# Transposing the result on VectorE, loading the up weights in two pieces, and starting the load buffers on a 4096-byte boundary

## The chip, the cores and the metric

The kernel runs on one core of one Trainium2 chip. The metric is the device time of one execution in microseconds (us). Each run also runs the kernel before on the same chip, in the same rounds. Ratios in this document are the mean time of one kernel's fast runs over the mean of the other's fast runs of the same rounds, so a ratio is not quite the ratio of the medians that are quoted. Intervals are 95%. The fast executions of one kernel scatter in two groups: in the rounds of the first four experiments the kernel before took 412.2 to 412.4 us seven times and 413.0 to 413.2 us four times. How many of each group a mean holds can move it by some tenths of a us.

Names in the profiles: PE is TensorE, the matrix engine, PEld its weight loads, DVE is VectorE, ACT ScalarE, POOL GpSimd, SP SyncE (here it issues the loads); a q after a name (SPq) is the queue of that engine. SBUF is the on-chip memory of 128 partitions into which the loads go, PSUM the memory into which PE writes. The granted clock is the share of TensorE's full clock that the throttle allowed.

## The reference

One decoding step of a transformer block for one token: attention over a long K/V cache, then a gated feed-forward layer. Everything is bf16 in memory.

```
x: (1, 1, 1024)   k_cache, v_cache: (1, 4, 65536, 128)   32 query heads, 4 K/V heads
wq: (1024, 4096)  wo: (4096, 1024)  w_gate, w_up: (1024, 3584)  w_down: (3584, 1024)

h  = x + attention(layernorm(x), k_cache, v_cache, wq, wo)
h2 = h + (gelu(layernorm(h) @ w_gate) * (layernorm(h) @ w_up)) @ w_down
```

The two caches are 134 MB of the 173 MB that have to be read, and each byte is used once. So the kernel can be no faster than its loads.

## The kernel before

All large loads go through one helper, into a rotating pool of five buffers of 32 KiB per partition, issued on one queue in the order of their use. A load can be issued when the load five places ahead of it has been used up.

```python
    CW = 16384
    NBUF = 5
    const = ctx.enter_context(tc.tile_pool(name="const", bufs=1))
    small = ctx.enter_context(tc.tile_pool(name="small", bufs=2))
    chpool = ctx.enter_context(tc.tile_pool(name="chpool", bufs=NBUF))
    # ... (cut)
    def load(src, name):
        t = chpool.tile([P, CW], BF16, name=name, tag="ch")
        n, w = src.shape[1], src.shape[2]
        tv = t[:, 0:n * w].rearrange("p (n w) -> p n w", w=w)
        nc.sync.dma_start(out=tv, in_=src)
        return tv
```

Pools lie in SBUF in the order in which they are opened. `const` and `small` come first, so the load buffers begin at byte 23552 of each partition (23 x 1024, or 5.75 x 4096). K is transposed on PE, bf16 pairs at a time as fp32, and multiplied with the queries; V is multiplied with the softmax.

```python
            for b in range(NB2):                                     # K, 4 transposes into one PSUM bank
                m0 = b * 8 + c * 2 + hf
                nc.tensor.transpose(out=kt_ps[:, b, :], in_=k32s[m0 // 16][:, m0 % 16, :], identity=ident_f[:])
            # ... (cut)
            nc.tensor.matmul(acc[32 * c:32 * c + rep * TG, :],       # V, 512 columns at a time
                             lhsT=pTs[a // HG][:, a % HG, :, :].rearrange("p r t -> p (r t)"),
                             rhs=v_sb[:, i * TG:(i + 1) * TG, :].rearrange("p t d -> p (t d)"), # ... (cut)
```

The last stages: the up weights are loaded in pieces of 4, 3 and 1 of the 8 row blocks, the down weights in pieces of 14, 7, 4, 2 and 1 of 28. The result lies as 128 partitions by 8 columns and has to become 8 rows of 128 for the store.

```python
    for j0, nj, src in up_proj(B_w_up, "wu", [GB] * (DC // GB - 1) + [GB - 1, 1]):    # 4, 3, 1
        # ... (cut)
    h2_cp = rows.tile([P, DC], F32, name="h2_cp")
    nc.vector.tensor_tensor(out=h2_cp[:], in0=dl_ps[:], in1=hd_cp[:], op=ALU.add)
    h2T_ps = ps_t.tile([DC, P], F32, name="h2T_ps", tag="T")
    nc.tensor.transpose(out=h2T_ps[:], in_=h2_cp[:], identity=ident_f[:])
    o_row = rows.tile([DC, P], BF16, name="o_row")
    nc.vector.tensor_copy(out=o_row[:], in_=h2T_ps[:])
    nc.sync.dma_start(out=out[0, 0].rearrange("(c p) -> c p", p=P), in_=o_row[:])
```

## Time and profile before

| | before |
|---|---|
| time, median of the first 3 runs | 412.27 us |
| span of the profiled run | 410.5 us |
| HBM bytes read, mean rate over the span | 173.02 MB, 422 GB/s |
| PE busy | 73% of the span |
| one 4 MiB load, mean from the first K landing to the last V landing | 9.82 us |
| last load landed | 406.9 us |
| last addition to issue of the store | 0.99 us |

These are lines of the page of the kernel before. In the strips each character is one of 40 equal slices; a digit is a busy share in tenths, PEclk the clock granted to TensorE, GB/s what the DMA engines moved.

```profile
span 410.5 us, 6349 instructions
PE 297.7 (73%) x2705; PEld 195.3 (48%) x2705; DVE 167.6 (41%) x292; ACT 168.0 (41%) x281; POOL 5.1 (1%) x16
...
DMA  8999999999999999999999999999999999999994
...
q8 instruction: 21, 0.34, 0.3%
...
HBM read 173.02 MB, written 0.00 MB: 422 GB/s over the span
```

DMA is at 9 in every slice but the first and the last, PE is not.

The next view is the chain of waits of the kernel before, from 300 us on: start, duration, and what the chain passed through.

```profile
311.41 25.09 DMA v_sb<-in_A_v_cache_dram
...
372.76 25.63 DMA wd_sb<-in_B_w_down_dram
398.39 0.04 issue
398.43 3.20 PE d_ps L358 x28
401.63 0.02 issue
401.66 0.70 DVE d_r L465
402.36 0.04 issue
402.40 1.86 PE hd_cp_ps L387 x8
404.27 3.06 PE dl_ps L460 x112
```

The last V load lands at 311.41 + 25.09 = 336.50 us and the first down-weight load at 398.39. From there PE is nearly always at work, and it finishes the narrow `dl_ps` matmuls at 407.33, a little after the last bytes land. Then comes the tail, here as the timeline shows it (start, duration, engine, line, operation):

```profile
407.35 0.17 DVE L468 TENSOR_TENSOR h_cp<-dl_ps,hd_cp 128x8 f32<-128x8 f32 x1 [2.87 <-PE dl_ps L460]
...
407.57 0.38 PE L470 MATMUL h2T_ps<-ident_f,h_cp 128*8 128x128 f32 x1 [0.26 <-DVE h_cp L468]
407.99 0.28 DVE L472 CAST o_row<-h2T_ps 8x128 bf16<-8x128 f32 x1 [0.47 <-PE h2T_ps L470]
408.34 0.35 SPq L473 DMA_DIRECT2D out_dram<-o_row  x1
```

### The profile page before, as it was taken

What the parts mean: (1) busy time and instruction counts of PE and PEld (TensorE: products, weight loads), DVE (VectorE), ACT (ScalarE), POOL (GpSimd) and SP (SyncE); (2) the same over time, 40 slices, a digit from 0 to 9 for tenths busy, and PEclk for the clock granted to TensorE, in tenths of its full rate; (3) what the DMA queues carried; (4) which work ended last, traced back from release to release, by engine and by line L of the source; (5) the groups of instructions that cost most, each with busy time, mean ns of one, the idle gap of its engine ahead of it and who ended that gap; (6) DMA issues with size and microseconds to landing.
All of it is one profiled execution on the core that took longest, in us unless ns stands there. A gap on an engine that the chain in (4) does not pass through costs nothing.

```text
span 410.5 us, 6349 instructions
## 1 busy us (share of the span) xinstructions
PE 297.7 (73%) x2705; PEld 195.3 (48%) x2705; DVE 167.6 (41%) x292; ACT 168.0 (41%) x281; POOL 5.1 (1%) x16
## 2 busy tenths in 40 slices
PE   0438989889688987496988929888987466466546
PEld 0216656655365654464565617465654223163225
DVE  0213565557256545265556535456545101021011
ACT  0013766653855654733655634455754700000000
POOL 1100000000000000000000000000000001000000
PEclk9986999999999999599999966999999585568565
DMA  8999999999999999999999999999999999999994
GB/s 358 409 460 407 460 408 457 407 454 414 439 428 429 434 417 449 416 449 410 449 420 441 423 441 426 431 433 426 437 426 437 422 445 422 434 430 433 429 418 174
DMA packets 6828, 173.43 MB, mean 422 GB/s; under 512 B 912, under 2 KB 912, under 8 KB 1296
## 3 DMA queue, kind: packets, MB, share of 16 engines
q1 hardware_dynamic: 6640, 173.02, 98.1%
q8 instruction: 21, 0.34, 0.3%
q14 instruction: 7, 0.06, 0.0%
q10 hardware_dynamic: 160, 0.00, 0.0%
HBM read 173.02 MB, written 0.00 MB: 422 GB/s over the span
## 4 chain that ended last, share of the span: by engine, by line
PE 51%; DMA 20%; DVE 14%; issue 8%; ACT 6%; POOL 0%; SPq 0%; POOLq 0%; ACTq 0%; DVEq 0%
PE kt_ps L220 26%; PE qk_ps L245 11%; DMA k_sb<-in_A_k_cache_dram 7%; DMA wd_sb<-in_B_w_down_dram 6%; DMA v_sb<-in_A_v_cache_dram 6%; DVE sc_sb L256 5%; PE acc_ps L300 5%; ACT pT L283 4%; PE sct_ps L253 4%; DVE mx L257 4%; DVE kt_sb L227 3%; ACT qk_sb L250 2%; PE o_ps L316 1%; PE wg_ps L160 1%; PE d_ps L358 1%
## 5 line engine op out<-in xcount | busy, mean ns | idle before, releaser
L220 PE MATMUL kt_ps<-ident_f,k_sb 128*128 128x128 f32 x1024 | 148.1, 288 | 17.4 <-DVE kt_sb L227 13.0
L225 ACT COPY kt_sb<-kt_ps 128x1024 bf16<-128x1024 bf16 x116 | 116.4, 1013 | 91.7 <-PE kt_ps L220 63.0
L220 PEld LDWEIGHTS kt_ps<-ident_f,k_sb 128*128 128x128 f32 x1024 | 117.5, 147 | 55.5 <-issue 21.3
L227 DVE COPY kt_sb<-kt_ps 128x1024 bf16<-128x1024 bf16 x140 | 94.6, 687 | 76.1 <-PE qk_ps L245 42.6
L245 PE MATMUL qk_ps<-kt_sb,qsel 128*32 128x512 bf16 x512 | 65.1, 395 | 7.7 <-DVE kt_sb L227 7.7
L256 DVE COPY sc_sb<-sct_ps 128x512 f32<-128x512 f32 x32 | 34.2, 1068 | 46.1 <-PE sct_ps L253 43.7
L283 ACT ACTIVATE pT<-sc_sb,nbias 128x256 bf16<-128x256 f32 x64 | 31.5, 493 | 20.6 <-DVE nbias L275 20.6
L300 PE MATMUL acc_ps<-v_sb,pT 128*32 128x512 bf16 x512 | 33.7, 407 | 3.7 <-DMA v_sb<-in_A_v_cache_dram 3.7
L250 ACT COPY qk_sb<-qk_ps 128x512 f32<-128x512 f32 x32 | 18.8, 589 | 24.9 <-PE qk_ps L245 16.5
L245 PEld LDWEIGHTS <-qsel 128*32 128x32 bf16 x512 | 15.1, 94 | 26.2 <-issue 23.8
L253 PE MATMUL sct_ps<-ident_f,qk_sb 128*128 128x128 f32 x128 | 19.9, 278 | 8.6 <-ACT qk_sb L250 8.6
L300 PEld LDWEIGHTS <-pT 128*32 128x32 bf16 x512 | 14.7, 102 | 18.5 <-issue 7.1
L257 DVE TENSOR_REDUCE mx<-sc_sb 128x8 f32<-128x512 f32 x32 | 22.0, 686 | 1.0
L253 PEld LDWEIGHTS sct_ps<-ident_f,qk_sb 128*128 128x128 f32 x128 | 14.3, 140 | 13.6 <-ACT qk_sb L250 13.6
L167 ACT COPY wg_ev<-wg_ps 96x512 f32<-96x512 f32 x1 | 0.6, 581 | 45.9 <-PE wg_ps L160 45.9
L309 PE MATMUL l_ps<-lpart,ones_f 128*128 128x8 f32 x16 | 3.7, 306 | 15.8 <-ACT pT L283 15.8
L358 PE MATMUL at_ps<-wo_sb,o2z 128*32 128x512 bf16 x64 | 7.1, 619 | 8.1 <-DMA wo_sb<-in_A_wo_dram 8.1
L160 PE MATMUL wu_ps<-wu_sb,hnz 128*32 128x512 bf16 x56 | 7.2, 625 | 7.8 <-DMA wu_sb<-in_B_w_up_dram 7.8
L160 PEld LDWEIGHTS <-hnz 128*32 128x32 bf16 x112 | 4.8, 123 | 16.0 <-issue 13.7
L283 ACT ACTIVATION_READ_ACCUMULATOR pT<-sc_sb,nbias 128x1 f32 x64 | 11.9, 187 | 0.0
L167 ACT ACT_TABLE_LOAD x1 | 1.3, 1283 | 25.0 <-DVE q_ev L165 25.0
L309 PEld LDWEIGHTS l_ps<-lpart,ones_f 128*128 128x128 f32 x16 | 3.0, 234 | 17.8 <-ACT pT L283 17.4
(126 smaller groups left out, 98.4 us busy)
## 6 DMA issues: line engine op xcount, KB each, us to landing
k_sb<-in_A_k_cache_dram SPq DMA_DIRECT2D x16, 4096.0 KB, 30.4
v_sb<-in_A_v_cache_dram SPq DMA_DIRECT2D x16, 4096.0 KB, 19.3
wq_sb<-in_A_wq_dram SPq DMA_DIRECT2D x2, 4096.0 KB, 16.7
wo_sb<-in_A_wo_dram SPq DMA_DIRECT2D x2, 4096.0 KB, 29.6
wg_sb<-in_B_w_gate_dram SPq DMA_DIRECT2D x2, 3584.0 KB, 36.4
wu_sb<-in_B_w_up_dram SPq DMA_DIRECT2D x1, 3584.0 KB
wd_sb<-in_B_w_down_dram SPq DMA_DIRECT2D x1, 3584.0 KB, 25.6
wu_sb<-in_B_w_up_dram SPq DMA_DIRECT2D x1, 2688.0 KB, 38.1
```

What stands on the lines that cost most here:

```text
L160: nc.tensor.matmul(banks[s // 4][32 * g:32 * g + 32, :], lhsT=stat, rhs=mov(s), start=first, stop=last, tile_position=(0, 32 * g))
L220: nc.tensor.transpose(out=kt_ps[:, b, :], in_=k32s[m0 // 16][:, m0 % 16, :], identity=ident_f[:])
L225: nc.scalar.copy(out=dst_bf, in_=src_bf)
L227: nc.vector.tensor_copy(out=dst_bf, in_=src_bf)
L245: nc.tensor.matmul(qk_ps[32 * c:32 * c + 32, :], lhsT=qsel[:, g, par, hf, :], rhs=mv[:, :, :, par], start=(hf == 0 and par == 0), stop=(hf ...
L250: nc.scalar.copy(out=qk_sb[:], in_=qk_ps[:])
L253: nc.tensor.transpose(out=sct_ps[:, b, :], in_=qk_sb[:, b * P:(b + 1) * P], identity=ident_f[:])
L256: nc.vector.tensor_copy(out=sl.rearrange("p h (m t) -> p m t h", t=2), in_=src_v)
L257: nc.vector.tensor_reduce(out=st["mx"][:, :, pi], in_=sl, axis=AX.X, op=ALU.max)
L283: nc.scalar.activation(out=pT[:, :, r, :], in_=sc_sb[:, r, hf * HG * TG:(hf + 1) * HG * TG].rearrange("p (a t) -> p a t", t=TG), func=ACT. ...
L300: nc.tensor.matmul(acc[32 * c:32 * c + rep * TG, :], lhsT=pTs[a // HG][:, a % HG, :, :].rearrange("p r t -> p (r t)"), rhs=v_sb[:, i * TG: ...
L358: nc.tensor.matmul(bank[32 * g:32 * g + 32, :], lhsT=stat, rhs=w2[:, s * 512:(s + 1) * 512], start=first, stop=last, tile_position=(0, 32 ...
```

## The change

It has three parts. The result is rounded to bf16 by the last addition, put into a zero-padded 128x32 block, and turned by four 32x32 transposes on VectorE, so that neither PE nor PSUM is needed in the tail. The up weights come in two loads of 4 row blocks. And a new pool `lead`, opened first and filled exactly to byte 20480 (5 x 4096), puts the load buffers, opened second, on a 4096-byte boundary of SBUF.

```diff
+    lead = ctx.enter_context(tc.tile_pool(name="lead", bufs=1))
+    ones_f = lead.tile([P, P], F32, name="ones_f")
     ... (14 more constant tiles move from const to lead)
+    chpool = ctx.enter_context(tc.tile_pool(name="chpool", bufs=NBUF))
     const = ctx.enter_context(tc.tile_pool(name="const", bufs=1))
     small = ctx.enter_context(tc.tile_pool(name="small", bufs=2))
-    chpool = ctx.enter_context(tc.tile_pool(name="chpool", bufs=NBUF))
     ... (cut)
-    for j0, nj, src in up_proj(B_w_up, "wu", [GB] * (DC // GB - 1) + [GB - 1, 1]):
+    for j0, nj, src in up_proj(B_w_up, "wu", [GB] * (DC // GB)):
     ... (cut)
+    o_blk = rows.tile([P, 32], BF16, name="o_blk")
+    nc.vector.memset(o_blk[:], 0.0)
+    o_tr = rows.tile([32, P], BF16, name="o_tr")
     ... (cut)
-    h2_cp = rows.tile([P, DC], F32, name="h2_cp")
-    nc.vector.tensor_tensor(out=h2_cp[:], in0=dl_ps[:], in1=hd_cp[:], op=ALU.add)
-    h2T_ps = ps_t.tile([DC, P], F32, name="h2T_ps", tag="T")
-    nc.tensor.transpose(out=h2T_ps[:], in_=h2_cp[:], identity=ident_f[:])
-    o_row = rows.tile([DC, P], BF16, name="o_row")
-    nc.vector.tensor_copy(out=o_row[:], in_=h2T_ps[:])
-    nc.sync.dma_start(out=out[0, 0].rearrange("(c p) -> c p", p=P), in_=o_row[:])
+    nc.vector.tensor_tensor(out=o_blk[:, 0:DC], in0=dl_ps[:], in1=hd_cp[:], op=ALU.add)
+    for i in range(4):
+        nc.vector.transpose(out=o_tr[:, 32 * i:32 * i + 32], in_=o_blk[32 * i:32 * i + 32, :])
+    nc.sync.dma_start(out=out[0, 0].rearrange("(c p) -> c p", p=P), in_=o_tr[0:DC, :])
```

More of the change, by code (lines that the diff above doesn't have):

```diff
@@ L58 @@
     assert NT % (DCH * CH) == 0 and CH % TG == 0 and CH == 32 and W2 == 16 and DCH % 2 == 0
+    lead = ctx.enter_context(tc.tile_pool(name="lead", bufs=1))
+    ones_f = lead.tile([P, P], F32, name="ones_f")
+    ident_f = lead.tile([P, P], F32, name="ident_f")
+    esel = lead.tile([P, 2, P], BF16, name="esel")
+    qsel = lead.tile([P, Hkv, 2, 2, 32], BF16, name="qsel")
+    hsel = lead.tile([P, 2], F32, name="hsel")
+    sel = lead.tile([P, 32], F32, name="sel")
+    x_pc = lead.tile([P, DC], F32, name="x_pc")
+    x_cp = lead.tile([P, DC], F32, name="x_cp")
+    x_row = lead.tile([DC, P], BF16, name="x_row")
+    ident_bf = lead.tile([P, P], BF16, name="ident_bf")
+    x_pc_bf = lead.tile([P, DC], BF16, name="x_pc_bf")
+    xn_bf = lead.tile([P, DC], BF16, name="xn_bf")
+    neg_half = lead.tile([P, 1], F32, name="neg_half")
+    oT_all = lead.tile([P, Hq], BF16, name="oT_all")
+    xnz = lead.tile([P, DC, 32], BF16, name="xnz")
+    chpool = ctx.enter_context(tc.tile_pool(name="chpool", bufs=NBUF))
     const = ctx.enter_context(tc.tile_pool(name="const", bufs=1))
     small = ctx.enter_context(tc.tile_pool(name="small", bufs=2))
-    chpool = ctx.enter_context(tc.tile_pool(name="chpool", bufs=NBUF))
     ps_m = ctx.enter_context(tc.tile_pool(name="ps_m", bufs=1, space=PSUM))
@@ L83 @@
     assert HD <= CW and DC % WB == 0
-    x_pc_bf = const.tile([P, DC], BF16, name="x_pc_bf")
     nc.scalar.dma_start(out=x_pc_bf[:], in_=A_x[0, 0].rearrange("(p c) -> p c", c=DC))
-    x_row = const.tile([DC, P], BF16, name="x_row")
     nc.scalar.dma_start(out=x_row[:], in_=A_x[0, 0].rearrange("(c p) -> c p", p=P))
@@ L91 @@
         wq_tiles.extend(wv[:, i, :] for i in range(WB))
-    ident_bf = const.tile([P, P], BF16, name="ident_bf")
     make_identity(nc, ident_bf[:])
-    ident_f = const.tile([P, P], F32, name="ident_f")
     make_identity(nc, ident_f[:])
-    ones_f = const.tile([P, P], F32, name="ones_f")
     nc.vector.memset(ones_f[:], 1.0)
-    hsel = const.tile([P, 2], F32, name="hsel")
     nc.vector.memset(hsel[:], 0.0)
@@ L102 @@
         nc.vector.memset(hsel[64 * s:64 * s + 64, s:s + 1], 1.0)
-    neg_half = const.tile([P, 1], F32, name="neg_half")
     nc.vector.memset(neg_half[:], -0.5)
-    sel = const.tile([P, 32], F32, name="sel")
     nc.vector.tensor_tensor(out=sel[:], in0=ident_f[:, 0:32], in1=ident_f[:, 32:64], op=ALU.add)
@@ L108 @@
     nc.vector.tensor_tensor(out=sel[:], in0=sel[:], in1=ident_f[:, 96:128], op=ALU.add)
-    esel = const.tile([P, 2, P], BF16, name="esel")
     for par in range(2):
@@ L140, in layernorm_cols @@
         nc.vector.tensor_scalar(out=dst_bf, in0=xc[:], scalar1=rstd[:, 0:1], scalar2=None, op0=ALU.mult)
-    x_pc = const.tile([P, DC], F32, name="x_pc")
     nc.vector.tensor_copy(out=x_pc[:], in_=x_pc_bf[:])
-    xn_bf = const.tile([P, DC], BF16, name="xn_bf")
     layernorm_cols(x_pc[:], xn_bf[:], "ln1")
@@ L147, with padded @@
     nc.tensor.transpose(out=xT_ps[:], in_=x_row[:], identity=ident_bf[0:DC, 0:DC])
-    x_cp = const.tile([P, DC], F32, name="x_cp")
     nc.vector.tensor_copy(out=x_cp[:], in_=xT_ps[:])
-    def padded(pool, vec, ncols, name):
-        t = pool.tile([P, ncols, 32], BF16, name=name)
+    def padded(pool, vec, ncols, name, t=None):
+        if t is None:
+            t = pool.tile([P, ncols, 32], BF16, name=name)
         nc.gpsimd.memset(t[:], 0.0)
@@ L170 @@
     assert NQ == 8 and D == 1024
-    xnz = padded(const, xn_bf[:], DC, "xnz")
+    padded(None, xn_bf[:], DC, "xnz", xnz)
     q_ps = [ps_qk.tile([P, 512], F32, name="q_ps", tag="qkps") for _ in range(2)]
@@ L185 @@
         nc.tensor.matmul(qsel_ps[:, par, :], lhsT=esel[:, par, :], rhs=qT_bf[:], start=True, stop=True)
-    qsel = const.tile([P, Hkv, 2, 2, 32], BF16, name="qsel")
     nc.vector.memset(qsel[:], 0.0)
@@ L192 @@
                                   in_=qsel_ps[64 * t:64 * t + 64, :, :].rearrange("p a (g h) -> p g a h", h=rep))
-    oT_all = const.tile([P, Hq], BF16, name="oT_all")
     k_v = [A_k_cache[0, g].rearrange("(p n) d -> p n d", p=P) for g in range(Hkv)]
```

## The prediction

> **What bounds the kernel.** The load stream. The page gives the 16 DMA engines 0.9 of every slice but the first and the last, 173.02 MB read at 422 GB/s over a span of 410.5 us. PE, the busiest compute engine, is busy 73%. Landings read from the chain of waits and from the DMA issues: the first K load (third in the queue) lands at 32.21 us, the last V load at 336.50, so 31 loads of 4 MiB took 9.82 us each (427 GB/s). The first down-weight load lands at 398.39: 428 GB/s all the way. The queue does not run dry: no V load took under 14.6 us from issue to landing, over one load's time. The Trainium skill, "DMA: Bandwidth & Descriptors", section "Where 436 GB/s comes from", puts the ceiling of the SBUF ports at 435.2 GB/s; this trace agrees: the wo loads landed 9.66 us apart (434 GB/s).
>
> **The tail.** The last 256 KB land near 406.9 (issue 391.5 plus 15.4). PE runs on to 407.33 (112 narrow matmuls in 3.2 us, clock 0.5). Then by the timeline: add at 407.35, PE transpose of the result 407.57 to 407.95, cast from PSUM 407.99 to 408.27, output DMA issued 408.34, span ends at 410.5.
>
> **What changes.**
> 1. Result transpose. Removed: a PE transpose (0.38 us) and the cast (0.28 us), with hand-overs 0.74 us, all on the critical path. Added: four independent 32x32 transposes on VectorE. Small DVE operations here last 0.16 to 0.18 us, and four independent casts of 64x64 took 0.93 us together, so my estimate is 0.4 to 0.6 us. Gain 0.15 to 0.35 us.
> 2. Up weights in 2 loads instead of 3: the bytes are the same. PE now has 28 matmuls (3.6 us at half clock) after the last up-weight bytes instead of 7, so act_bf comes about 2 us later, near 395.5 instead of 393.6, still ahead of the down weights at 398.4. The first down-weight load is issued near 359 instead of 372.76, but behind the same bytes, so it lands no earlier. Gain 0 to 0.1 us.
> 3. Load buffers begin at byte 20480 (5 x 4096) per partition instead of 23552 (5.75 x 4096). It can only matter through the rate of the DMA writes. The old start is already a multiple of 1024, and wo ran at 434 GB/s into the same unaligned buffers, so a large cost of misalignment is not visible. Upper bound: all K and V loads at 9.66 instead of 9.82 us, 32 x 0.16 = 5 us. Most likely nothing, with a fair chance of 1 to 3 us; 0.7 us on average.
>
> **Predicted time:** 411.0 us, 408.2 to 412.4 eight times in ten. Faster by over 2% (under 404.0) 0.03, within 2% 0.95, slower by over 2% 0.02.
>
> **What would show it.** Step 1: last add to output issue about 0.7 us instead of 1.0. Step 2: wd landings keep their distance to the last V landing; the last wu matmul ends near 393.5. Step 3: the time per 4 MiB load between the first K and the last V landing: 9.82 us if alignment is nothing, 9.70 or less if it counts.
>
> **What would make it wrong.** The DMA write rate depends on the 4096-byte boundary more than wo's rate suggests (gain of 3 to 5 us); a transpose on DVE costs over 0.3 us each in sequence; the later act_bf pushes the last stage past the wd landing.

## The result, and the profile after

The changed kernel took 412.36 us (median of 6 runs, 412.15 to 412.73), the kernel before 412.35 us (median of 6, 412.17 to 413.30). The ratio is 0.9997, interval 0.9984 to 1.001: no difference.

The page after the change, the lines that answer to those of before:

```profile
span 410.4 us, 6350 instructions
PE 296.6 (72%) x2704; PEld 194.9 (47%) x2704; DVE 168.2 (41%) x296; ACT 168.0 (41%) x281; POOL 5.1 (1%) x16
...
DMA  8999999999999999999999999999999999999994
...
q8 instruction: 21, 0.34, 0.3%
```

The load stream is the same. The first K load landed at 32.15 us and the last V load at 336.60, so a 4 MiB load took 304.45 / 31 = 9.82 us on average, to the hundredth what it took before. In both traces 1.213 us is the median time of one 32 KiB DMA packet. Two lines of the chain of waits after the change show the first K load (before: `1.65 30.56`) and the first down-weight load:

```profile
1.64 30.51 DMA k_sb<-in_A_k_cache_dram
...
359.31 38.93 DMA wd_sb<-in_B_w_down_dram
```

The timeline of the last stages after the change:

```profile
389.82 3.51 PE L165 MATMUL wu_ps<-wu_sb,hnz 128*32 128x512 bf16 x28 [5.04 <-DMA wu_sb<-in_B_w_up_dram]
...
395.04 0.20 DVE L444 TENSOR_TENSOR act_bf<-wu_t,gl 128x12 bf16<-128x12 f32 x1
398.29 3.18 PE L361 MATMUL d_ps<-wd_sb,actz 128*32 128x512 bf16 x28 [3.28 <-DMA wd_sb<-in_B_w_down_dram]
...
407.22 0.17 DVE L473 TENSOR_TENSOR o_blk<-dl_ps,hd_cp 128x8 bf16<-128x8 f32 x1 [2.89 <-PE dl_ps L466]
407.42 0.84 DVE L475 STREAM_TRANSPOSE o_tr<-o_blk 32x32 bf16<-32x32 bf16 x4
408.34 0.36 SPq L476 DMA_DIRECT2D out_dram<-o_tr  x1
```

Two things are to be seen. The up matmuls now end at 389.82 + 3.51 = 393.33 and the activation is ready at 395.24, about 1.6 us later than before (393.63), but PE still has to wait for the down weights until 398.29, so this costs nothing. And the four transposes take 0.84 us. The tail from the last addition to the store's issue is 408.34 - 407.22 = 1.12 us, where it was 0.99: it became longer by 0.13 us, and the store goes out at the same 408.34 us because in this run the first down weights were used 0.14 us earlier (398.29 against 398.43).

The chain of waits after the change shows how the four transposes follow one another (in the place of the second one the chain has 0.21 us of VectorE's own queue):

```profile
407.22 0.18 DVE o_blk L473
407.40 0.02 issue
407.42 0.20 DVE o_tr L475
407.62 0.21 DVEq L502
407.83 0.01 issue
407.85 0.20 DVE o_tr L475
408.05 0.01 issue
408.06 0.20 DVE o_tr L475
```

Each lasts 0.20 us and the next starts when the one before is over. They do not overlap, although none depends on another.

### The profile page after: what moved, and what is told of

It is laid out like the page before. It is cut to its first block, busy times and chain, and to the rows that moved or that the text cites. A ratio compares the mean times of both kernels' runs of the same rounds, so it can differ in the third digit from the quotient of the medians.

```text
span 410.4 us, 6350 instructions
## 1 busy us (share of the span) xinstructions
PE 296.6 (72%) x2704; PEld 194.9 (47%) x2704; DVE 168.2 (41%) x296; ACT 168.0 (41%) x281; POOL 5.1 (1%) x16
## 3 DMA queue, kind: packets, MB, share of 16 engines
q1 hardware_dynamic: 6496, 173.02, 98.1%
HBM read 173.02 MB, written 0.00 MB: 422 GB/s over the span
## 4 chain that ended last, share of the span: by engine, by line
PE 52%; DMA 24%; DVE 14%; ACT 7%; issue 2%; SPq 0%; DVEq 0%; ACTq 0%
PE kt_ps L223 27%; PE qk_ps L248 11%; DMA wd_sb<-in_B_w_down_dram 9%; DMA k_sb<-in_A_k_cache_dram 7%; DMA wo_sb<-in_A_wo_dram 7%; DVE sc_sb L259 6%; PE acc_ps L303 5%; ACT pT L286 5%; PE sct_ps L256 4%; DVE mx L260 4%; DVE kt_sb L230 3%; ACT qk_sb L253 2%; PE at_ps L361 1%; PE o_ps L319 1%; PE d_ps L361 1%
```

## The experiments

The theory at this point: the null result is the sum of a layout that does nothing, a load count that does next to nothing, and a tail that is 0.13 us longer. The rival: the parts have effects that cancel. The first four runs take the parts apart and push the layout the other way.

### The layout alone

```diff
 (the changed kernel, with this undone)
-    for j0, nj, src in up_proj(B_w_up, "wu", [GB] * (DC // GB)):
+    for j0, nj, src in up_proj(B_w_up, "wu", [GB] * (DC // GB - 1) + [GB - 1, 1]):
 (and with the PE transpose in the tail, as before)
```

> Only the layout of the change: load buffers from byte 20480, three up-weight loads and the PE transpose as before. Theory (the start address does not matter, the null result is three nulls): ratio to before 1.000 +-0.001, last V load at 336.5 +-0.2 us, wo loads 9.6 to 9.7 us apart. Rival (the layout gains 0.3 us or more and the other two parts give it back): 0.3 us or more faster than before, first down-weight load landing before 398.1.

Measured: 412.32 us median of 5, ratio 0.9992 (0.9979 to 1.0005). The profiled run was the slowest of its five (413.15 us), with its last down-weight load at 407.69 us, so its landings say nothing about a gain; its two wo loads landed 9.66 us apart, and its median packet took 1.213 us, as before and after the change. The theory holds: no gain or loss of the layout can be seen. The interval still allows a gain of up to 0.2%.

### Two up-weight loads alone

```diff
-    for j0, nj, src in up_proj(B_w_up, "wu", [GB] * (DC // GB - 1) + [GB - 1, 1]):
+    for j0, nj, src in up_proj(B_w_up, "wu", [GB] * (DC // GB)):
```

> Only the up weights in 2 loads. Theory: the first down-weight load lands 0.05 to 0.25 us earlier than the 398.4 of before, because one load with its 128 short packets is gone, and the whole run is 0 to 0.25 us faster, within noise of before; act_bf ready near 395. Rival (the 2 loads are what costs, by starving the queue or making PE late): first down-weight landing later than 398.5 or the last stage starting later than its landing, run slower by 0.3 us or more.

Measured: 412.22 us median, ratio 0.9994 (0.9981 to 1.0006). One execution, the profiled one, took 893.8 us with a granted clock of 1.0; it is left out, and so there is no profile to read landings from. (Its trace shows what was slow: PE was busy for 835.7 of 892.0 us, and one K transpose took 686 ns where it took 288 in the kernel before, while VectorE's largest group of copies took 692 ns each against 687. The trace holds no throttle record at all, so the clock of 1.0 says nothing of what PE got.) The run called "bf16 in the PE transpose" below has the same two loads: there the first down weights were used at 398.44 us and the last load landed at 406.92, against 398.43 and 406.9 before. So the 0.14 us by which the changed kernel's landings were earlier in its profile is within what traces differ by, and not shown to be a gain of the two loads. The rival (the two loads cost 0.3 us or more) is not supported.

### The VectorE transposes alone

```diff
+    o_blk = rows.tile([P, 32], BF16, name="o_blk")
+    nc.vector.memset(o_blk[:], 0.0)
+    o_tr = rows.tile([32, P], BF16, name="o_tr")
 ... (and the tail of the change)
```

> Only the four VectorE transposes of the result. Theory: four transposes one after another at 0.21 us, from last add to output issue 1.12 us instead of 0.99, so 0.1 to 0.15 us slower, which the timed runs will hardly resolve. Rival (the tail gains 0.15 to 0.35 us as predicted, and the traced run was a bad one): 0.65 to 0.85 us from last add to output issue.

Measured: 1.12 us from the last addition (407.47) to the store's issue (408.59), as in the changed kernel, so the rival falls:

```profile
407.47 0.17 DVE L470 TENSOR_TENSOR o_blk<-dl_ps,hd_cp 128x8 bf16<-128x8 f32 x1 [3.81 <-PE dl_ps L463]
407.67 0.84 DVE L472 STREAM_TRANSPOSE o_tr<-o_blk 32x32 bf16<-32x32 bf16 x4
408.59 0.36 SPq L473 DMA_DIRECT2D out_dram<-o_tr  x1
```

The time was 413.18 us median of 6, ratio 1.0018 (1.0002 to 1.0034): slower by 0.75 us in the mean, more than the 0.13 us that the tail explains. The six runs spread from 412.58 to 414.88 us, the spread of the kernel before in the same rounds is 412.23 to 413.16. The changed kernel has the same tail and is not slower than before, so the rest of this difference is not put down to the transposes; what it is stays open.

### The buffers 32 bytes off

```diff
     xnz = lead.tile([P, DC, 32], BF16, name="xnz")
+    pad = lead.tile([P, 16], BF16, name="pad")
+    nc.gpsimd.memset(pad[:], 0.0)
     chpool = ctx.enter_context(tc.tile_pool(name="chpool", bufs=NBUF))
```

> The changed kernel with its load buffers pushed 32 bytes on, to byte 20512, so that no load row begins on a multiple of 256 (or 1024, or 4096) any more. Theory that the start address never matters to the DMA writes: same as the changed kernel within 0.1%. Rival (boundaries matter, but before was already on a multiple of 1024, which is enough): [...]1 to 3 us slower, loads 9.7 to 9.75 us apart instead of 9.66.

Measured: 414.48 us median of 5 (414.41 to 414.53), ratio 1.0045 (1.0033 to 1.0057). So the start address does matter, and my theory that it never does falls; the rival, that boundaries matter but that the old start was already good enough, is what remains. In the timeline of this run the first down weights are used 2.05 us later than in the changed kernel (400.34 against 398.29), so the loss is in the load stream. The landings agree with the expected 9.7 to 9.75 us: the median step from one 4 MiB load to the next is 9.72 us here and 9.67 before and after the change.

```profile
400.34 3.18 PE L363 MATMUL d_ps<-wd_sb,actz 128*32 128x512 bf16 x28 [3.08 <-DMA wd_sb<-in_B_w_down_dram]
...
409.67 0.84 DVE L477 STREAM_TRANSPOSE o_tr<-o_blk 32x32 bf16<-32x32 bf16 x4
410.59 0.37 SPq L478 DMA_DIRECT2D out_dram<-o_tr  x1
```

### The buffers 64 and 256 bytes off

The same edit with a pad of 32 and of 128 bf16 elements. These two ask which boundary it is.

> The changed kernel with its load buffers 64 bytes on (byte 20544). The run with 32 bytes on was 0.45% slower than before. Theory (a row that begins off a multiple of 256[...]): slower by 1.5 to 2.5 us, as with 32. Rival (only a multiple of 64 is needed): within 0.4 us of before.

> The changed kernel with its load buffers 256 bytes on (byte 20736, a multiple of 256 but of neither 1024 nor 4096). Theory (256 is enough): within 0.4 us of before. Rival (1024 is needed, which before had and this one lacks): slower by 1 to 2.5 us as with 32.

Measured: with 64 bytes 414.19 us median of 5 (414.06 to 414.25), ratio 1.0032 (1.0020 to 1.0044); with 256 bytes 412.74 us median of 6, ratio 1.0000 (0.9987 to 1.0013). So 64 is not enough, and 256 is enough. The median step between loads is 9.72 us with 64 bytes, the same as with 32, and 9.67 with 256. Whether 64 costs less than 32 is not shown: against the kernel before it lost 1.3 us in the mean and 32 lost 1.9, but those are other rounds on another chip, and the two medians are 0.3 us apart. Both 20480 and the old 23552 are multiples of 256, and moving from one to the other did nothing. Offsets of 128 were not tried.

The Trainium skill, "DMA: Bandwidth & Descriptors", section "How a descriptor splits into AXI transactions", says that a transaction must start from a 256-byte-aligned address, and that for a descriptor which does not start there the first transaction starts at the boundary below, so that bytes are fetched which are not used. The page tells this of reading; these runs show a cost of such starts on the side that writes to SBUF, but not that it arises in this way. They also give the size: 1.9 us over 173.02 MB in rows of 32 KiB on 16 engines (330 rows for each) is about 6 ns a row, an estimate from those numbers; the step of 9.72 us instead of 9.67 for 8 rows on each engine gives the same.

### One VectorE transpose instead of four

A 128x32 block is four 32x32 blocks one under another, so one instruction can turn all four. Then the result lies in four groups of 8 partitions, and takes four stores.

```diff
-    for i in range(4):
-        nc.vector.transpose(out=o_tr[:, 32 * i:32 * i + 32], in_=o_blk[32 * i:32 * i + 32, :])
-    nc.sync.dma_start(out=out[0, 0].rearrange("(c p) -> c p", p=P), in_=o_tr[0:DC, :])
+    nc.vector.transpose(out=o_tr[:], in_=o_blk[:])
+    out_v = out[0, 0].rearrange("(c i q) -> i c q", i=4, q=32)
+    for i in range(4):
+        eng = nc.sync if i % 2 == 0 else nc.scalar
+        eng.dma_start(out=out_v[i], in_=o_tr[32 * i:32 * i + DC, :])
```

> The changed kernel with one VectorE transpose of 128x32 in place of four of 32x32, and four output DMAs of 8 rows of 64 bytes, two on each of two queues. Theory (each transpose instruction costs a fixed 0.2 us and the four do not overlap): the one instruction lasts 0.2 to 0.25 us, so 0.6 us of the tail goes; the second issue on each queue gives back about 0.35 us; last add to last output issue 0.75 to 0.9 us instead of 1.12. Rival (the 0.84 us is the time of the 4096 elements): one instruction of 0.8 us. Total time within 0.3 us of before either way.

The timeline of that run:

```profile
408.88 0.17 DVE L473 TENSOR_TENSOR o_blk<-dl_ps,hd_cp 128x8 bf16<-128x8 f32 x1 [2.91 <-PE dl_ps L466]
409.08 0.21 DVE L474 STREAM_TRANSPOSE o_tr<-o_blk 128x32 bf16<-128x32 bf16 x1
409.33 0.64 ACTq L478 DMA_DIRECT2D out_dram<-o_tr  x2
409.37 0.70 SPq L478 DMA_DIRECT2D out_dram<-o_tr  x2
```

One instruction over all 128 partitions lasts 0.21 us, hardly more than one over 32 (0.20). So the 0.84 us was the cost of four instructions, not of 4096 elements, and the theory holds. (Both forms have 32 elements in each partition; shorter or longer rows were not tried.) The four stores give most of it back: two issues on one queue take 0.70 us, and the last is issued 0.90 us after the addition. Time 412.55 us median of 4, ratio 0.9994 (0.9966 to 1.0021), not to be told from before.

### bf16 in the PE transpose, with the two loads

```diff
-    h2_cp = rows.tile([P, DC], F32, name="h2_cp")
+    h2_cp = rows.tile([P, DC], BF16, name="h2_cp")
     nc.vector.tensor_tensor(out=h2_cp[:], in0=dl_ps[:], in1=hd_cp[:], op=ALU.add)
-    h2T_ps = ps_t.tile([DC, P], F32, name="h2T_ps", tag="T")
-    nc.tensor.transpose(out=h2T_ps[:], in_=h2_cp[:], identity=ident_f[:])
+    h2T_ps = ps_t.tile([DC, P], BF16, name="h2T_ps", tag="T")
+    nc.tensor.transpose(out=h2T_ps[:], in_=h2_cp[:], identity=ident_bf[:])
```

> Candidate for a better version, right result: the kernel before with the up weights in 2 loads, the result rounded to bf16 by the last add, and PE transposing bf16 instead of fp32. Theory: the PE transpose falls from 0.38 us to about 0.15, last add to output issue 0.75 us instead of 0.99; first down-weight load 0.05 to 0.25 us earlier than 398.4; together 0.3 to 0.5 us, ratio about 0.999, hardly resolved by the timed runs. Rival (transpose time is fixed cost): 0.95 us or more from add to issue.

The timeline of the tail:

```profile
407.37 0.17 DVE L468 TENSOR_TENSOR h_cp<-dl_ps,hd_cp 128x8 bf16<-128x8 f32 x1 [2.89 <-PE dl_ps L460]
...
407.59 0.27 PE L470 MATMUL h2T_ps<-ident_bf,h_cp 128*8 128x128 bf16 x1 [0.26 <-DVE h_cp L468]
407.90 0.21 DVE L472 COPY o_row<-h2T_ps 8x128 bf16<-8x128 bf16 x1 [0.36 <-PE h2T_ps L470]
408.18 0.36 SPq L473 DMA_DIRECT2D out_dram<-o_row  x1
```

From addition to issue 0.81 us, against 0.99 before and 1.12 in the change. The transpose fell from 0.38 to 0.27 us, less than I expected, and the copy from 0.28 to 0.21. The check finds the result correct, but it finds that also of the two runs below that are wrong, so it proves little. The time was 412.18 us median of 6, ratio 0.9981 (0.9958 to 1.0003). This is the best tail of the three, but a faster kernel is not shown: the interval includes 1, and 0.18 us of the tail is 0.04% of the time.

### What keeps the stream at 428 GB/s

The prediction left room for a gain because the mean load took 9.82 us and the wo loads 9.66. The layout was one suspect for those 0.16 us, and it is now cleared. The traces hold a hint. The landing intervals of single loads (issue plus time to landing, one load to the next) are not all 9.8: in the kernel before, most of the 31 are 9.5 to 9.9 and three are near 10.9, and these three hold 3.7 of the 4.8 us that the 31 take beyond 9.66 us each. The second K load landed 10.90 us after the first, and the third 9.67 us after that. These are the DMA lines of the kernel before for the windows 33 to 43 us and 43 to 53 us (packets, MB, share of 16 engines):

```profile
q1 hardware_dynamic: 147, 4.29, 99.8%
q8 instruction: 1, 0.02, 0.5%
...
q1 hardware_dynamic: 144, 4.19, 97.1%
```

An instruction transfer lies in the long interval and none in the short one. The Trainium skill, "Runtime: NRT & Kernel Launch", section "Instruction fetch mechanics", says that instructions come by DMA in blocks of 16 KiB, 256 instructions each. PE executes 2705 matmuls and 2705 weight loads, 5410 instructions or 21.1 such blocks, and the trace has 21 transfers. The theory for the next runs: such a transfer delays one of the 16 DMA engines, and as each load waits for its slowest engine, delays add up on that engine.

Fewer PE instructions, first try (wrong result):

```diff
-            for b in range(NB2):
-                m0 = b * 8 + c * 2 + hf
-                nc.tensor.transpose(out=kt_ps[:, b, :], in_=k32s[m0 // 16][:, m0 % 16, :], identity=ident_f[:])
+            m0 = c * 8 + c * 2 + hf
+            nc.tensor.matmul(kt_ps[:], lhsT=k32s[m0 // 16][:, m0 % 16, :],
+                             rhs=ident_f[:].unsqueeze(1).to_broadcast([P, NB2, P]), start=True, stop=True)
```

> Wrong result on purpose: the kernel before, but each four 128-column transposes of K become one 512-column matmul, so PE executes 1536 instructions fewer of 5410 with about the same streaming time. Question: what holds the stream at 427 to 428 GB/s when single loads run at 434? Theory: the fetch of PE instructions (21 transfers of 16 KB on the instruction queue) delays single DMA engines, and the slowest engine sets the landings: 15 or 16 such transfers, 0.6 to 1.5 us faster, fewer landing intervals of about 11 us. Rival (the steps come from something else, HBM or the row pitch): instruction transfers fall, the time stays within 0.3 us of before.

This was a miss: 451.76 us, ratio 1.0927. In this run each fp32 matmul of 512 columns was two instructions of 592 ns (512 of them for 256 matmuls, so only 1024 PE instructions fewer, and 17 transfers), PE was busy for 381.5 us instead of 297.7, and it became the bound. It tells nothing about instruction transfers.

More PE instructions (right result): each V matmul of 512 columns as four of 128.

```diff
-            nc.tensor.matmul(acc[32 * c:32 * c + rep * TG, :], ..., rhs=v_sb[:, i * TG:(i + 1) * TG, :]...)
+            for t in range(TG):
+                nc.tensor.matmul(acc[32 * c:32 * c + rep * TG, t * Dh:(t + 1) * Dh], ..., rhs=v_sb[:, i * TG + t, :], ...)
```

> Right result: the kernel before, but each 512-column matmul on V is four of 128 columns, so PE executes 3072 instructions more, with the same streamed columns. Theory (instruction fetch delays the slowest DMA engine): 33 transfers of 16 KB instead of 21, 1 to 2.5 us slower, more landing intervals of about 11 us. Rival: 33 transfers, time within 0.3 us of before. If PE became the bound instead, loads would wait for PE and come over 15 us late; then the run tells nothing on the question.

Measured: 417.18 us, ratio 1.0098 (1.0078 to 1.0119), with 33 instruction transfers. But the DMA strip of this run has a 7 in the eleventh slice of 40, which holds 111 us, where it should have 9, so the load queue ran short there once, and the 4.1 us are not instruction traffic alone (a division follows below):

```profile
DMA  8999999999799999999999999999999999999993
...
q8 instruction: 33, 0.54, 0.5%
```

Again, with the split kept out of the first V group:

```diff
-            for t in range(TG):
-                nc.tensor.matmul(acc[..., t * Dh:(t + 1) * Dh], ...)
+            for t in range(TG if g >= 1 else 1):
+                n = 1 if g >= 1 else TG
+                nc.tensor.matmul(acc[..., t * Dh:(t + n) * Dh], ...)
```

> Right result: as the run with more PE instructions, but only for the last three of the four V groups, since in that run the load queue ran empty once in the first, near 111 us. 2304 PE instructions more. Theory: about 30 transfers on the instruction queue, 0.8 to 1.8 us slower than before, no DMA slice under 0.9 in the middle. Rival: 30 transfers, within 0.3 us of before.

Measured: 414.90 us median of 6 (413.76 to 415.79), ratio 1.0046 (1.0029 to 1.0063), 30 instruction transfers. The strip shows no slice under 9 any more, but a closer look does: in the 10.4 us from 256.5 us the DMA share was 0.90, where the kernel before has 1.00, so a part of these 1.9 us is again a queue that ran short (see below). The profiled run was the slowest of the six.

Fewer PE instructions, second try (wrong result), in bf16:

```diff
-            for b in range(NB2):
-                m0 = b * 8 + c * 2 + hf
-                nc.tensor.transpose(out=kt_ps[:, b, :], ...)
+            m0 = c * 8 + c * 2 + hf
+            k_bf = k32s[m0 // 16][:, m0 % 16, :].bitcast(BF16)[:, 0:P]
+            nc.tensor.matmul(kt_ps[:], lhsT=k_bf, rhs=ident_bf[:].unsqueeze(1).to_broadcast([P, NB2, P]),
+                             start=True, stop=True)
```

> Wrong result on purpose, a second try at fewer PE instructions after the fp32 one made PE the bound: four fp32 transposes of K become one 512-column bf16 matmul, 1536 PE instructions fewer of 5410, PE less busy. Theory (instruction fetch delays the slowest DMA engine): about 15 transfers on the instruction queue, 0.6 to 1.5 us faster than before, the first down-weight load before 397.8. Rival (the landing steps of 11 us come from something else): 15 transfers, within 0.3 us of before.

Measured: 411.03 us median, ratio 0.9962 (0.9947 to 0.9977): faster by 1.6 us in the mean. The profiled execution took 1003.21 us at a granted clock of 1.0 and is left out, as in the run with two loads, so landings can't be read. Its count of instruction transfers can:

```profile
q8 instruction: 15, 0.25, 0.1%
```

This agrees with the theory: 6 transfers fewer, and by far the largest gain, on a kernel whose loads are the same bytes. It does not isolate it: PE also had less to do, and the two runs in the other direction were mixed with a short queue. So the times alone do not settle it.

The kept traces do, for the mechanism. Their files hold more than the views print: start and duration of every DMA packet, and for each load 16 landing marks, taken here as one for each DMA engine; the views give only the last mark. Three things stand in the trace of the kernel before:

- A 32 KiB data packet takes 1.213 us (98.8% of 4608). While such packets run, 18 instruction transfers of 16 KiB come by, and each of the 18 overlaps a data packet of 1.67 to 1.76 us (one of them two more long ones). After the first 3 us only 6 other such packets take over 1.5 us, two of them beside instruction transfers of 8 KiB. Moved by 3 to 8 us, the same 18 times meet only 0 to 2 of them. In the changed kernel it is 18 of 18 again.
- At the second K load 15 of the 16 marks lie between 41.49 and 41.88 us, and one, behind the transfer that started at 36.36, at 43.11. It is as late at the third load (51.16 to 51.52, and 52.77): the delay stays.
- The delays add up. The 16 marks of the first K load span 0.39 us, those of the last load 4.03 us (402.86 to 406.89). A transfer costs time when it meets the engine that is last, or makes another one last; each of the three intervals near 10.9 us holds a transfer.

So an instruction transfer delays the engine that carries it by about 1.2 us, and the load stream ends with its most delayed engine. An estimate of what all such delays cost here is at most 3.6 us: the 4.03 us between the first and the last mark at the end, less the 0.39 at the start. The same marks divide the two losses: with 33 transfers the first mark of the last load came at 406.03 and the last at 411.76, so the least delayed engine was 3.2 us later than before (the short queue) and the spread 1.7 us wider; with 30 transfers it was 406.17 and 410.32, 3.3 us later and a spread wider by only 0.1. The loss in that profile is therefore nearly all short queue, and the run is no support for the theory. What part of the gain with 15 transfers comes from the transfers and what part from a PE with less to do stays open, since no fast profile of it exists.

## Why the prediction was right or wrong

The measured 412.36 us lies in the stated range of 408.2 to 412.4, and "within 2%" with 0.95 was right. That it lies inside is partly luck: the range ends 0.05 us above the time of the kernel before (412.35), and two of the six executions (412.52 and 412.73) lie outside. The forecast gain of 1.3 us did not come.

- **What bounds the kernel: right.** DMA is at 9 in every slice but the first and the last, before and after. The experiments that moved the time by more than 1 us were those that touched the load stream or the load on PE; of the three that changed the tail, the traces show differences of 0.1 to 0.2 us, which the times do not resolve (the 0.75 us of the run with the transposes alone is more than that, and unexplained).
- **Step 1, the tail: wrong in size, and so in sign.** The term that was mis-sized is "my estimate is 0.4 to 0.6 us" for the four transposes. They took 0.84 us: each lasts 0.20 us, and the next starts when the one before is over. The removed part was 0.74 us as stated. So instead of gaining 0.15 to 0.35 us the tail lost 0.13. The evidence was at hand: the four independent casts in the same profile took 0.93 us together, and I wrote that number down and then estimated half of it. The run with one instruction showed that the number of instructions is what costs: 128x32 takes 0.21 us and 32x32 takes 0.20.
- **Step 2, two loads: right.** The last up matmul ended at 393.33 (predicted 393.5), the activation was ready at 395.24 (395.5), the first down-weight load was issued at 359.31 (359), and its landing moved by no more than 0.14 us, which other traces do not confirm.
- **Step 3, the layout: the likeliest outcome was right, the average was not.** "Most likely nothing" held, with 9.82 us per load before and after, the figure named for that case. The "fair chance of 1 to 3 us" was a mistake that the skill could have prevented: the section on transactions named above gives 256 bytes, and the old start, which I knew to be a multiple of 1024, satisfied it. The upper bound of 5 us was worked out from the 0.16 us between mean and best loads, as if misalignment were the only thing that could cause them. The landing marks put them elsewhere: on the engines that instruction transfers delayed.

So nothing speaks for a cancellation of large effects. In the traces the layout gives 0, the tail costs 0.13 us, the two loads give 0.14 us or less, and the sum is under the scatter of the runs, which is about 1 us. The times of the single parts are less sharp than that: that of the layout allows a gain of 0.2%, and the 0.75 us of the tail alone stay open.

## What to carry to other kernels

Before moving buffers to a rounder boundary, check whether they break the one that counts: here the three starts that are multiples of 256 bytes did equally well, and 32 or 64 bytes off cost 0.3 to 0.45%. Cost small operations in a serial tail by the number of instructions, at about 0.2 us each here, not by the partitions they cover; replacing two instructions by four is then a loss even when the four are tiny and independent. When the loads bound the kernel and run at nearly full rate, what is left may lie in traffic that is not data, so look at the instruction lines of the DMA queues too, and ask of each load not only when it landed but how far apart its DMA engines finished.

## What the Trainium skill lacked or had wrong

- "VectorE: DVE Perf Modes", section "The three transpose paths", gives 311 ns for a 128x128 bf16 block on VectorE, and its section "Rules for kernel authors" calls the VectorE transpose the fastest for 32x32. Neither says what one small block costs: 0.199 us for 32x32 and 0.21 us for 128x32, with four in a row taking 0.84 us.
- "DMA: Bandwidth & Descriptors", section "How a descriptor splits into AXI transactions", tells the 256-byte rule and counts its price in beats (transfers of 32 bytes) of short descriptors; it does not give the price in time for loads of long rows into SBUF: 0.45% of the whole time at 32 bytes off, 0.32% at 64, nothing at 256.
- "Runtime: NRT & Kernel Launch", section "Instruction fetch mechanics", calls the cost of crossing a 16 KiB block "mostly hidden". Its block size agrees with this trace (21 transfers for 5410 PE instructions, 15 with 1536 fewer). The section does not mention that these transfers delay the loads: here each of 18 met a data packet of about 1.7 us instead of 1.213, and the engines of the last load finished 4.03 us apart. The kernel with 15 transfers was 1.6 us faster; how much of that is theirs is not isolated.
- No page that I read tells of executions like the two here that took 893.8 and 1003.2 us, among others of 412 and 411 us of the same kernels. In both PE was busy for 94% of the span (835.7 and 937.0 us), while the trace holds no throttle record and the clock reads 1.0.
